# Splitting a load of 127 rows into 112 and 15 in a fused attention, Fourier and MLP kernel

## The chip, the cores and the metric

The kernel runs on one NeuronCore of a Trainium2 chip. The metric is the device time of one execution in microseconds (us). TensorE is called PE, VectorE DVE, ScalarE ACT, GpSimd POOL. SyncE, called SP, computes nothing here: it issues most of the DMA transfers, one after the other, in the order in which the program lists them. A transfer is carried out by the core's 16 DMA engines, and a semaphore tells the waiting engines when it has landed.

## The reference, cut to what matters

Three blocks follow each other: attention with a learned relative bias, a Fourier mixing block with an MLP, and a gated block. Only the hand-over from attention to the Fourier transform is touched here.

```python
attn = softmax(q @ k.T / 8 + bias) @ v                 # B=4, 8 heads, S=576, D=64
x = attn.transpose(0, 2, 1, 3).reshape(4, 576, 512)
X = np.fft.fft(np.fft.fft(x, axis=1), axis=2)          # over the sequence, then over the width
u = x + np.real(X)
un = (u - mean(u)) / sqrt(var(u) + 1e-6)
x = u + relu(un @ w_ch1) @ w_ch2                       # 512 -> 2048 -> 512
# then: w_in, a normalisation, a 576 x 576 spatial product, a gate, w_out
```

All of it is float32 with split products (a high and a low part), so a matrix product takes several matmuls.

## The kernel before, in words

The program runs in stages: the bias (up to about 130 us), attention (130 to 390 us), the Fourier stage (388 to 459 us), the MLP with its normalisation, and the gated block, which ends at 1096 us.

Attention takes the 16 pairs (4 batches, 4 pairs of heads) in order, two pairs at a time in nine steps `d`, each step two units of 128 query rows. A step computes scores on PE (L417), adds the bias on DVE, takes the exponential on ACT (L453), and then turns the probabilities round so that they can be multiplied with the values on PE (L519, tile `po`). In odd steps (and the last four) PE turns them (L493). In even steps ACT and POOL make a half-precision copy `hl` (L464, L470) and SP issues a DMA transpose of it (L483, `pt<-hl`), three steps before PE reads the result. SP also issues the loads of `q`, `k` and `v` (L382, tile `raw`) and the stores of the finished rows to a buffer in HBM, `xd[b]`, one of 576 rows by 512 for each batch: `store` issues one transfer for rows 0 to 511 (L569) and two for the last 64 rows (L572).

The Fourier transform of a real sequence over 576 positions needs only sums and differences of row `t` and row `576 - t`, so each batch is loaded from `xd[b]` in such a way that these rows share a partition. `Folds.loads` does this for one batch: POOL writes zeros, and then SP issues six transfers (L748), rows 0 to 127 and 128 to 255 into slots 0 and 1, the 127 rows from 256 into slot 3 from partition 1 on, 128 rows from 383 into slot 4, one row, and the last 64 rows into slot 2. A row is 2048 bytes. The tile is `x` for batch 0, `raw` for batch 1 and `lowb` for batches 2 and 3.

When the loads go out is set in `first_folds`. Batch 0's go out one by one during attention: `after(n)` is called at the end of each step with `n` counted from the last one, and in the steps that `F_STEPS` names it takes one step of the generator. Batch 1's go out together at `n = 0` and batch 2's at `n = 3`. Batch 3's are the operation `load` in the Fourier stage, behind the first three weight loads (L1697, tile `w`); SP has to wait there until the last stores to `xd[3]` have landed.

In the Fourier stage a planner (`Plan.run`) fixes the order of each engine's operations from written-down durations. For each batch DVE makes the sums (L765, L776, L783, "folds"), PE multiplies them with cosines and sines (L878, tile `y`), ACT copies the result out of PSUM (L882), PE applies the second transform (L908, tile `D`), and DVE adds (L918, L926). Between these ACT and DVE also prepare the first MLP weights: ACT scales a weight tile (L1036, `wsq<-w`) as soon as its load has landed, and in ACT's list the first of these stands ahead of two of the copies L882. The planner counts batch 3's load as one operation of 6 us on SP, whatever it is made of.

Of the kernel before, what the change touches and what calls it, by code (L numbers as in the profile page):

```python
# [713 lines left out]
class Folds:  # L714
# [22 lines left out]
    def loads(self, b):  # L737
        nc, x, d = self.nc, self.xs[b], self.xd[b]
        f = slice(1, DM + 1)

        def zeros():
            if b == 0:
                nc.gpsimd.memset(x[64:128, 2], 0.0)
            nc.gpsimd.memset(x[:, 2, 0 : DM + 2 : DM + 1], 0.0)
            nc.gpsimd.memset(x[0:1, 3, f], 0.0)

        def part(p, k, lo, n):
            nc.sync.dma_start(out=x[p : p + n, k, f], in_=d[lo : lo + n])  # L748

        yield zeros  # L750
        for p, k, lo, n in (0, 0, 0, 128), (0, 1, 128, 128), (1, 3, 256, 127), (0, 4, 383, 128), (64, 2, 511, 1), (0, 2, 512, 64):
            yield lambda p=p, k=k, lo=lo, n=n: part(p, k, lo, n)

    def load(self, b):
# [39 lines left out]
def first_folds(folds):  # L794

    todo, loads = [], folds.loads(0)

    def after(n):
        if F_LOAD <= n < 0 and n % 9 in F_STEPS:
            next(loads, int)()  # L800
        if n == 0:
            folds.open()
            todo.extend(folds.steps(0))
        if n in X_LOAD:
            folds.load(1 + X_LOAD.index(n))
        for _ in range(FOLDS.get(n, 0)):
            todo.pop(0)[2]()

    return after
# [1125 lines left out]
```

## Time and profile before

| | us |
|---|---|
| median of 3 runs | 1096.97 (1095.49 to 1101.35) |
| the profiled execution | 1098.06 |
| its span in the trace | 1096.3 |
| PE busy in the span | 1017.9 (93%) |
| DVE, ACT, POOL busy | 692.5, 546.2, 293.6 |

The span is the time between the first and the last instruction in the trace; the execution's own time is 1.76 us longer. The profile page gives each engine's busy time over the whole span, which is an average over stages that have different limits. So the rows further down are taken stage by stage: from the timeline (instructions of one engine in order of time), from tables of busy time by window, and from the chain of waits, which follows the end of the program back to what released each step. A number in square brackets at the end of a timeline row is the idle time of the engine ahead of that row, with what ended it.

### The profile page before, as it was taken

The numbers are of one execution on the slowest core, as the hardware profiler recorded it, in microseconds if no ns is written. First come the engines' busy times: TensorE is split into PE (matmuls) and PEld (weight loads), VectorE is DVE, ScalarE is ACT, GpSimd is POOL, SyncE is SP. The second block draws the span as 40 slices with busy tenths as digits, with TensorE's granted clock in tenths as the row PEclk, the third lists the DMA queues.
The fourth block names the chain that finished last, engine by engine and source line by source line (L and its number), as shares of the span: only waits on it lengthen the run. The fifth ranks groups of instructions, "written<-read, shape, count | busy, mean of one in ns | idle before, by whom it ended". The sixth has DMA issues, their size and how long they took to land.

```text
span 1096.3 us, 25413 instructions
## 1 busy us (share of the span) xinstructions
PE 1017.9 (93%) x10547; PEld 928.3 (85%) x10547; DVE 692.5 (63%) x1812; ACT 546.2 (50%) x1034; POOL 293.6 (27%) x284
## 2 busy tenths in 40 slices
PE   6989888888688979999999999999999999999998
PEld 3777777877678856789999999999999989988897
DVE  5999888888678877877875332433792366261611
ACT  3888698888679734644531121211452234333322
POOL 2767786878569300000000000000003020110000
PEclk7999989999889989999999999999999999999999
DMA  4542057889787641134520000000241000101011
GB/s 165 176 138 83 14 125 160 179 186 161 177 167 152 136 139 42 39 102 135 173 94 1 1 2 1 1 1 20 78 162 28 1 1 1 39 1 49 1 39 48
DMA packets 116167, 88.22 MB, mean 80 GB/s; under 512 B 85840, under 2 KB 96340, under 8 KB 116052
## 3 DMA queue, kind: packets, MB, share of 16 engines
q1 hardware_dynamic: 113184, 79.82, 28.8%
q10 hardware_dynamic: 2724, 5.90, 1.6%
q8 instruction: 82, 1.34, 0.5%
q0 software_dynamic: 144, 0.89, 0.2%
q14 instruction: 33, 0.27, 0.1%
HBM read 57.10 MB, written 9.44 MB: 61 GB/s over the span
## 4 chain that ended last, share of the span: by engine, by line
PE 65%; DVE 14%; POOL 8%; issue 5%; DMA 4%; ACT 3%; SPq 1%; ACTq 0%; POOLq 0%; DVEq 0%
PE h L1360 18%; PE acc L1396 18%; PE psp L1532 5%; PE pu L1507 4%; PE po L1554 4%; POOL hl L470 4%; PE pv L1455 3%; DVE mask L243 2%; PE po L519 2%; DVE bt L320 2%; PE turn L493 2%; PE bps L276 2%; PE sc L417 2%; DMA lowb<-xd 1%; DVE pt L502 1%
## 5 line engine op out<-in xcount | busy, mean ns | idle before, releaser
L1364 ACT ACTIVATE gh<-h 128x256 fp32r<-128x256 f32 x144 | 54.9, 381 | 243.1 <-PE h L1360 239.2
L1365 DVE SCALAR_TENSOR_TENSOR gl<-h,gh 128x256 fp32r<-128x256 f32 x144 | 60.9, 423 | 171.3 <-ACT gh L1364 170.7
L1360 PE MATMUL h<-uh,wh 128*128 128x256 f32 x576 | 161.7, 281 | 2.2 <-DVE gl L1365 2.0
L1396 PE MATMUL acc<-gh,wh 128*128 128x256 f32 x576 | 163.1, 283 | 0.0
L1396 PE MATMUL acc<-gh,wl 128*128 128x256 f32 x576 | 161.1, 280 | 1.4 <-DVE wl L1068 1.4
L1360 PE MATMUL h<-uh,wl 128*128 128x256 f32 x576 | 161.0, 280 | 1.0 <-DVE wl L1068 1.0
L1360 PE MATMUL h<-ul,wh 128*128 128x256 f32 x576 | 160.8, 279 | 0.0
L1396 PE MATMUL acc<-gl,wh 128*128 128x256 f32 x576 | 160.8, 279 | 0.0
L1152 POOL MEMSET w<- 64x288 f32 x2 | 0.7, 334 | 443.3 <-DVE wsq L1049 443.3
L1360 PEld LDWEIGHTS h<-uh,wh 128*128 128x128 f32 x576 | 109.1, 189 | 3.0 <-DVE gl L1365 2.4
L1396 PEld LDWEIGHTS acc<-gh,wl 128*128 128x128 f32 x576 | 108.5, 188 | 1.7 <-DVE wl L1068 1.6
L1360 PEld LDWEIGHTS h<-uh,wl 128*128 128x128 f32 x576 | 108.5, 188 | 1.2 <-DVE wl L1068 1.2
L1396 PEld LDWEIGHTS acc<-gh,wh 128*128 128x128 f32 x576 | 108.9, 189 | 0.4
L1396 PEld LDWEIGHTS acc<-gl,wh 128*128 128x128 f32 x576 | 108.9, 189 | 0.3
L1360 PEld LDWEIGHTS h<-ul,wh 128*128 128x128 f32 x576 | 108.8, 189 | 0.0
L453 ACT ACTIVATE P<-s,mm 128x576 f32<-128x576 f32 x144 | 103.4, 766 | 3.9 <-DVE mm L445 3.6
L519 PE MATMUL po<-vp,pt 128*128 128x65 f16 (+3 forms) x2324 | 85.4, 197 | 8.3 <-DMA pt<-hl 7.0
L519 PEld LDWEIGHTS <-pt 128*128 128x128 f16 (+1 forms) x2324 | 81.9, 102 | 11.9 <-DMA pt<-hl 7.7
L470 POOL TENSOR_TENSOR hl<-P,hl 128x1024 f16<-128x1024 f32 x68 | 86.1, 1287 | 19.2 <-ACT hl L464 12.6
L493 PE MATMUL turn<-ident,P 128*128 128x128 f32 x380 | 58.9, 287 | 28.6 <-DVE pt L502 28.1
L276 PE MATMUL bps<-g,mask 128*128 128x64 f16 x1152 | 63.1, 196 | 16.2 <-DVE lowb L310 8.3
L493 PEld LDWEIGHTS turn<-ident,P 128*128 128x128 f32 x380 | 41.8, 144 | 41.5 <-DVE pt L502 15.8
(256 smaller groups left out, 2598.5 us busy)
## 6 DMA issues: line engine op xcount, KB each, us to landing
w<-in_w_ch SPq DMA_DIRECT2D x32, 512.0 KB
vld<-in_v ACTq DMA_DIRECT2D x16, 320.0 KB
raw<-in_q SPq DMA_DIRECT2D x16, 320.0 KB
raw<-in_v SPq DMA_DIRECT2D x16, 320.0 KB
raw<-in_k SPq DMA_DIRECT2D x16, 288.0 KB
xd<-x SPq DMA_DIRECT2D x16, 256.0 KB
w<-in_w_in SPq DMA_DIRECT2D x8, 512.0 KB
out<-o SPq DMA_DIRECT2D x16, 256.0 KB
```

The lines of the kernel that those rows point to most:

```text
L276: nc.tensor.matmul(out=full(ps, it // 2)[:, it % 2, :, gi], lhsT=ms[gi][:, 128 * it + 64 * (it // 2) :][:, 0:128], rhs=g[:, k], start=(k = ...
L453: nc.scalar.activation(out=P[:, x, 0:S], in_=s, func=AF.Exp, bias=mm[:, 1, x : x + 1], scale=1.0)
L470: nc.gpsimd.tensor_tensor(out=hl[:, :, o : o + c], in0=P[:, :, j : j + c], in1=hl[:, :, j : j + c], op=ALU.subtract)
L493: nc.tensor.transpose(t[:, 128 * k : 128 * k + 128], P[:, 128 * k : 128 * k + 128], ident)
L519: nc.tensor.matmul(out=po[c, t % 4, 0:w], lhsT=pt[:, x, c], rhs=vp[:, j, hh, f : f + w], start=(i == 0), stop=(i == len(seq) - 1),)
L1360: nc.tensor.matmul(out=h, lhsT=st[:, q], rhs=mv[:, k], start=(n == 0), stop=(n == 11))
L1364: nc.scalar.activation(out=gh, in_=h, func=AF.Relu)
L1365: nc.vector.scalar_tensor_tensor(out=gl, in0=h, scalar=0.0, in1=gh.bitcast(F32), op0=ALU.max, op1=ALU.subtract)
L1396: nc.tensor.matmul(out=acc[x, d // 2][:, d % 2], lhsT=st[:, q], rhs=mv, start=(e == 0 and d % 2 == 0 and n == 0), stop=(e == NF - 1 and d ...
L1507: nc.tensor.matmul(out=p[:, 0:CH], lhsT=st[:, q], rhs=mv[:, kk, e], start=(n == 0), stop=(n == 11))
L1532: nc.tensor.matmul(out=p[:, 0:CH], lhsT=st, rhs=mv, start=(n == 0), stop=(n == len(seq) - 1))
L1554: nc.tensor.matmul(out=p, lhsT=st[:, f, c], rhs=mv, start=(n == 0), stop=(n == 11))
```

## The change

The list of transfers in `Folds.loads` gets one more entry. The 127 rows from row 256 on go as 112 rows (256 to 367, into partitions 1 to 112) and 15 rows (368 to 382, into partitions 113 to 127). The bytes, their places and the other transfers stay.

```diff
         yield zeros
-        for p, k, lo, n in (0, 0, 0, 128), (0, 1, 128, 128), (1, 3, 256, 127), (0, 4, 383, 128), (64, 2, 511, 1), (0, 2, 512, 64):
+        parts = (0, 0, 0, 128), (0, 1, 128, 128), (1, 3, 256, 112), (113, 3, 368, 15), (0, 4, 383, 128), (64, 2, 511, 1), (0, 2, 512, 64)
+        for p, k, lo, n in parts:
             yield lambda p=p, k=k, lo=lo, n=n: part(p, k, lo, n)
```

The order of PE, DVE, ACT and POOL stays as it was. SP gets four more transfers. For batch 0 the generator has one more element, so everything behind the 112 rows goes out one place later. In the middle of attention SP's order was this (`x_71` is batch 0's tile, `xd_74` its buffer in HBM):

```order
L483 DMA_TRANSPOSE pt<-hl 128x18x128
L748 DMA x_71<-xd_74 127x512
L748 DMA x_71<-xd_74 128x512
L483 DMA_TRANSPOSE pt<-hl 128x18x128
L382 DMA raw<-in_k 128x576
L382 DMA raw<-in_q 128x640
L569 DMA xd_75<-x 128x4x128
L572 DMA xd_75<-x 64x64 x2
L483 DMA_TRANSPOSE pt<-hl 128x18x128
L382 DMA raw<-in_v 128x640
L748 DMA x_71<-xd_74 1x512
```

With the change the same place reads:

```order
L483 DMA_TRANSPOSE pt<-hl 128x18x128
L748 DMA x_71<-xd_74 112x512
L748 DMA x_71<-xd_74 15x512
L483 DMA_TRANSPOSE pt<-hl 128x18x128
L382 DMA raw<-in_k 128x576
L382 DMA raw<-in_q 128x640
L569 DMA xd_75<-x 128x4x128
L572 DMA xd_75<-x 64x64 x2
L483 DMA_TRANSPOSE pt<-hl 128x18x128
L382 DMA raw<-in_v 128x640
L748 DMA x_71<-xd_74 128x512
L483 DMA_TRANSPOSE pt<-hl 128x18x128
```

The 15 rows stand where the next 128 rows stood; those go out some steps later in the single row's place, and the single row and the last 64 rows move back in the same way.

At the end of attention and the start of the Fourier stage SP's order was this (`xd_76` and `xd_77` are the buffers of batches 2 and 3, `w` the weight tiles):

```order
L748 DMA lowb<-xd_76 128x512 x2
L748 DMA lowb<-xd_76 127x512
L748 DMA lowb<-xd_76 128x512
L748 DMA lowb<-xd_76 1x512
L748 DMA lowb<-xd_76 64x512
L569 DMA xd_77<-x 128x4x128
L572 DMA xd_77<-x 64x64 x2
L1697 DMA w_8645<-in_w_ch 128x1024
L1697 DMA w_8648<-in_w_ch 128x1024
L1697 DMA w_8650<-in_w_ch 128x1024
L748 DMA lowb<-xd_77 128x512 x2
L748 DMA lowb<-xd_77 127x512
```

With the change:

```order
L748 DMA lowb<-xd_76 128x512 x2
L748 DMA lowb<-xd_76 112x512
L748 DMA lowb<-xd_76 15x512
L748 DMA lowb<-xd_76 128x512
L748 DMA lowb<-xd_76 1x512
L748 DMA lowb<-xd_76 64x512
L569 DMA xd_77<-x 128x4x128
L572 DMA xd_77<-x 64x64 x2
L1698 DMA w_8648<-in_w_ch 128x1024
L1698 DMA w_8651<-in_w_ch 128x1024
L1698 DMA w_8653<-in_w_ch 128x1024
L748 DMA lowb<-xd_77 128x512 x2
```

Here nothing changes places; each load has one transfer more, in the place of the 127 rows.

## Rows read from the trace of the kernel before

**Rows 1.** Busy time by window: Fourier stage, then everything behind it.
```profile
398.20:459.00 60.80, 55.97 (x256) 38.94 (x255) 42.53 (x80) 30.59 (x60) 0.00 (x0) 0.94 0.23 74
459.00:1096.30 637.30, 624.42 (x4751) 600.77 (x4749) 316.61 (x768) 208.35 (x487) 32.84 (x31) 1.00 0.13 42
```
**Rows 2.** Same view (PE, PEld, DVE, ACT, POOL, granted clock, DMA share, GB/s).
```profile
412.00:414.00 2.00, 2.00 (x9) 1.51 (x8) 0.12 (x1) 0.81 (x2) 0.00 (x0) 0.83 0.82 217
416.00:420.50 4.50, 4.50 (x23) 2.63 (x21) 0.71 (x2) 0.96 (x2) 0.00 (x0) 1.00 0.07 25
274.00:278.00 4.00, 1.45 (x16) 1.05 (x12) 3.06 (x8) 3.90 (x7) 2.93 (x4) 1.00 0.07 25
```
**Rows 3.** Timeline of SP in attention: start, duration, line, operation, tiles, count.
```profile
236.75 0.57 SPq L748 DMA_DIRECT2D x<-xd  x1
...
263.67 2.76 SPq L483 DMA_TRANSPOSE pt<-hl  x1
266.48 3.80 SPq L748 DMA_DIRECT2D x<-xd  x2
270.45 9.22 SPq L483 DMA_TRANSPOSE pt<-hl  x1
```
**Rows 4.** Timeline of PE in attention, around its longest wait.
```profile
269.97 1.03 PE L519 MATMUL po<-vp,pt 128*128 128x65 f16 x28 [0.28 <-DMA pt<-hl]
...
272.53 1.08 PE L519 MATMUL po<-vp,pt 128*128 128x65 f16 x30
...
281.76 1.71 PE L519 MATMUL po<-vp,pt 128*128 128x65 f16 x28 [6.31 <-DMA pt<-hl]
...
286.26 1.14 PE L519 MATMUL po<-vp,pt 128*128 128x65 f16 x30
```
**Rows 5.** Timeline of PE: the same matmul of four nine-step rounds in turn.
```profile
229.65 0.38 PE L417 MATMUL sc<-kh,qh 128*128 128x288 f32 x1
...
260.55 0.38 PE L417 MATMUL sc<-kh,qh 128*128 128x288 f32 x1
...
297.74 0.38 PE L417 MATMUL sc<-kh,qh 128*128 128x288 f32 x1
...
330.05 0.38 PE L417 MATMUL sc<-kh,qh 128*128 128x288 f32 x1
```
**Rows 6.** Timeline of SP from the end of attention on.
```profile
383.57 10.48 SPq L748 DMA_DIRECT2D lowb<-xd  x6
394.14 0.53 SPq L569 DMA_DIRECT2D xd<-x  x1
...
397.82 5.41 SPq L1697 DMA_DIRECT2D w<-in_w_ch  x3
...
405.20 5.53 SPq L748 DMA_DIRECT2D lowb<-xd  x1
```
**Rows 7.** The chain of waits, 385 to 500 us: start, duration, what.
```profile
394.14 9.86 DMA xd<-x
...
405.20 15.74 DMA lowb<-xd
```
**Rows 8.** Timelines of DVE (first three) and ACT (last), Fourier stage.
```profile
391.75 0.68 DVE L548 TENSOR_TENSOR x<-po,ri 128x512 f32<-128x512 f32 x1
...
403.00 1.23 DVE L765 TENSOR_TENSOR lowb<-lowb 128x1024 f32<-128x1024 f32 x1 [4.75 <-DMA lowb<-xd]
...
421.13 1.22 DVE L765 TENSOR_TENSOR lowb<-lowb 128x1024 f32<-128x1024 f32 x1 [4.43 <-DMA lowb<-xd]
...
405.36 0.66 ACT L1036 ACTIVATE wsq<-w 128x512 f32<-128x512 f32 x1 [7.56 <-DMA w<-in_w_ch]
```
**Rows 9.** Timeline of PE, Fourier stage.
```profile
406.38 3.27 PE L878 MATMUL y<-tt,F 128*128 128x290 f32 x6 [3.50 <-ACT y L882]
409.44 3.72 PE L908 MATMUL D<-y,fs 128*128 128x290 f32 x8
...
415.93 2.12 PE L908 MATMUL D<-y,fs 128*128 128x290 f32 x8
...
426.95 1.74 PE L878 MATMUL y<-tt,F 128*128 128x290 f32 x6
```

## The prediction

> **What bounds the kernel now.** I read the windows by stage first, then the timelines of SP and PE in the two stretches where the loads of L748 go out, then the chain of waits. Behind 459 us PE is busy 624.4 of 637.3 us [rows 1], and nothing there reads the loaded rows: that part can only move as a whole. What can be won lies ahead of it, where PE waits.
>
> The windows show what the 127 rows do. In 416 to 420.5 us, when batch 3's load is under way, the DMA engines are busy 7% of their time and move 25 GB/s, and in 274 to 278 us, after batch 0's, the same [rows 2]. One of 16 engines is 6.25%. So in these stretches one engine works alone, at 25 GB/s. 127 rows of 2048 bytes are 260,096 bytes: at 25 GB/s 10.4 us. While transfers of 128 rows pass, between 412 and 414 us, the share is 0.82 and the rate 217 GB/s. I conclude that the 127 rows go through one engine in a single line, and that whatever else has a part on that engine stands behind them.
>
> Two stretches show the price. In attention SP issues the 127 rows at 266.48 us, and the two transfers there take 3.80 us of its time, against 0.57 for a plain one; the DMA transpose behind them holds SP for 9.22 us, against 2.76 for the one before [rows 3]. PE then stands 6.31 us for a transposed tile [rows 4]. At the start of the Fourier stage the chain of waits runs through a store of 9.86 us and a load of 15.74 us, with nothing but a little issue between them [rows 7]. The store was issued at 394.14 us, behind the six transfers of batch 2's load, which took SP 10.48 us [rows 6], though the rows it stores were ready at 391.75 + 0.68 = 392.43 us [rows 8].
>
> **The change part by part.** Durations are those of the profiled execution, 1098.06 us; the median is 1.09 us lower, and I subtract the same gain from it.
>
> First, how the two new transfers go. No row shows 112 or 15 rows. On one engine 112 rows would take 112 x 2048 bytes / 25 GB/s = 9.2 us, on sixteen a sixteenth, 0.6 us. The nearest rows are the transfers of 128 rows, spread out, and 112 is a multiple of 16 as 128 is; I take 0.6 us. The 15 rows take 1.2 us on one engine and 0.1 us on fifteen, and neither matters below.
>
> The Trainium skill says so outright, in "DMA: Bandwidth & Descriptors", section "Why a DMA increments its semaphore by 16 and not by 1": a transfer is split over the largest number of engines, up to 16, that divides its slowest dimension, so 127 partitions get one, and by the same rule 112 get 16 and 15 get 15. The trace agrees for 127 (a share of 0.07). The same page's "Rules for kernel authors" speaks against this change: two transfers to disjoint parts of the partitions are not worth it, since both share the 16 engines, and one transfer should be used. By that rule the time would stay at 1097 plus four more issues; the 25 GB/s of rows 2 is why I give it little.
>
> Attention, batch 0. The wait of 6.31 us goes, and with it the slow clock behind it: from 281.76 to 286.26 us PE does in 4.50 us what it does from 269.97 to 272.53 in 2.56 us [rows 4], 1.94 us more. Together 8.25 us is the upper end. The lower end comes from the length of a round, taken at the same matmul: 30.90, 37.19 and 32.31 us [rows 5]. Against the longer neighbour the disturbed one is 4.9 us too long, against the mean of both 5.6. Half way between 5.6 and 8.25 I take 6.9 us. What is late next is what sets the ordinary rounds, PE, ACT and POOL by turns.
>
> What the change adds there: one issue, at most 0.6 us of SP by the plain transfer in rows 3. Batch 0's later parts move one place back, ahead of other transposes. Each costs SP what it cost in its old place, and they land long before the Fourier stage reads them. The 0.6 us lie beside POOL's and ACT's work on the next transpose's input, since a transpose holds SP for only 2.76 us and one comes every second step, of some 3.5 us (a ninth of a round); uncovered they would cost 0.6 us.
>
> Fourier stage, batches 1 to 3. In the changed kernel seven transfers of batch 2 take SP about 7 x 0.57 = 4.0 us instead of 10.48, so SP is ready before the last rows are (392.43 us). The three stores and three weight issues follow until about 396 us; batch 3's seven transfers are out at about 401 and landed at about 403. DVE comes to batch 2's first fold right after batch 1's last, at about 398.3 us, instead of 403.00: its wait of 4.75 us goes. Its wait of 4.43 us for batch 3 [rows 8] goes too, since DVE cannot be there before 408 (421.13 less both waits and the slow stretch below), and the data are. ACT's wait of 7.56 us for the first weights shrinks to almost nothing, because the weight load is issued some 3.5 us earlier and has no part behind a line of 127 rows.
>
> What this is worth is decided on PE, which is busy in nearly all of the rest of the stage. There its wait of 3.50 us goes (it came from the copy L882 that stood behind ACT's wait), and the slow clock behind it: 3.27 instead of 1.74 us for six matmuls, 3.72 instead of 2.12 for eight [rows 9], 3.13 us in all. That is 6.63 us. The upper end is DVE's two waits, 9.18 us, if PE's smaller waits behind DVE close as well; the lower end is PE's wait alone, 3.50 us, if the clock falls anyway. I take half way between 6.63 and 9.18, 7.9 us. PE then bounds the stage: it is busy 55.97 of 60.80 us [rows 1], and the 4.83 us left over and the 3.13 us make 7.96, about what I take. The four added issues lie on SP, which then waits for the stores and not they for it.
>
> Sum: 6.9 + 7.9 = 14.8 us. 1098.06 - 14.8 = 1083.3 for a profiled execution, 1096.97 - 14.8 = 1082.2 for the median. I forecast 1082.
>
> **The rivals.**
> *Attention takes its gain back.* Rounds are set by several engines in turn, and the two behind the stall may be short only because others had caught up. For it: ordinary rounds differ by 1.4 us too [rows 5], so something else than the stall has its say. Against: the neighbours on both sides are alike [rows 5]. Then only the Fourier stage gains: 1096.97 - 7.9 = 1089.
> *The Fourier stage takes its gain back,* because the weights or batch 3's rows still come late (SP issues everything in one line). For it: SP's three weight issues take 5.41 us [rows 6]. Against: that time was spent behind the same engine. Then 1096.97 - 6.9 = 1090.
> *The change does not do what it says:* 112 rows go through one engine as well, 9.2 us instead of 10.4. Rows 2 do not exclude it. Between 1092 and 1099, say 1097.
> *Slower: SP is held by the number of transfers it has outstanding, not by the one engine.* The place is the transfer behind the 127 rows: it holds SP 5.53 us [rows 6] and, in attention, the greater part of 3.80. If a new transfer is held whenever a few are open, a seventh in each load is one more hold: 3.80 - 0.57 = 3.2 us ahead of the transpose in attention and 5.53 us ahead of the stores and in batch 3's load, 3.2 + 2 x 5.53 = 14 us less what lies beside other work, about 11: 1108. It decides from the point where a transfer behind the 15 rows holds SP for more than 3 us. Against it: transfers one behind another elsewhere take 0.6 us each.
>
> **How the numbers follow.** Forecast 0.73, attention alone failing 0.10, the Fourier stage alone failing 0.08, no effect 0.05, slower 0.04. The likeliest case's own bounds are 1096.97 - 17.4 = 1079.5 (both upper ends) and 1096.97 - 8.4 = 1088.6 (both lower ends). The range takes in the first two rivals and, below, another 3.5 us for waits of PE that the rows do not tell apart: 1076 to 1090. A measurement of this kernel can tell about 0.5%, 5.5 us, from no change. Below 1091.5 lie the first three cases, 0.91, less 0.01 for their edges: faster 0.90. The case of no effect and the edges give 0.06 for the same, and the last 0.04 is slower.
>
> **What would show it.** In the profile of the changed kernel no window of some microseconds should be left with a DMA share of 0.07 and 25 GB/s around the loads; no DMA transpose should hold SP over 4 us; the third round in rows 5 should last about 30 us; DVE's two waits for `lowb<-xd` should be gone and ACT's for `w` be under 2 us; PE's first MLP matmul, at 459 us before, should start about 15 us earlier, and the time from there to the end should be the same. I am wrong if the 112 rows still show 25 GB/s, if the transfer behind the 15 rows holds SP, or if the MLP's start moves by less than 9 us.

## The result and the profile after

The changed kernel takes 1076.78 us (median of 4 runs, 1075.67 to 1081.53) against 1096.23 us (4 runs, 1094.3 to 1101.35) measured beside it. The ratio is 0.9832 with a 95% interval of 0.9808 to 0.9856, so 15.8 to 21.0 us less. The forecast was 1082, range 1076 to 1090: the right direction and the right places, but the gain was about 19 us where 14.8 were forecast.

The lines of SP in attention that answer to [rows 3], timeline view:

```profile
263.01 2.78 SPq L483 DMA_TRANSPOSE pt<-hl  x1
265.84 1.10 SPq L748 DMA_DIRECT2D x<-xd  x2
267.12 3.19 SPq L483 DMA_TRANSPOSE pt<-hl  x1
```

The two transfers take 1.10 us in place of 3.80, and the transpose behind them holds SP for 3.19 us in place of 9.22. The longest of all 34 transposes holds it for 3.79. PE's timeline, which answers to [rows 4], has no wait for a transposed tile any more, except 0.28 us that were there before:

```profile
269.32 1.03 PE L519 MATMUL po<-vp,pt 128*128 128x65 f16 x28 [0.28 <-DMA pt<-hl]
...
271.88 1.08 PE L519 MATMUL po<-vp,pt 128*128 128x65 f16 x30
...
274.66 1.02 PE L519 MATMUL po<-vp,pt 128*128 128x65 f16 x28
...
277.34 1.08 PE L519 MATMUL po<-vp,pt 128*128 128x65 f16 x30
```

The same matmul of four rounds in turn, as in [rows 5]:

```profile
228.72 0.38 PE L417 MATMUL sc<-kh,qh 128*128 128x288 f32 x1
...
259.90 0.38 PE L417 MATMUL sc<-kh,qh 128*128 128x288 f32 x1
...
288.77 0.38 PE L417 MATMUL sc<-kh,qh 128*128 128x288 f32 x1
...
319.16 0.38 PE L417 MATMUL sc<-kh,qh 128*128 128x288 f32 x1
```

The rounds last 31.18, 28.87 and 30.39 us, where they lasted 30.90, 37.19 and 32.31: 8.32 us less in the disturbed one.

At the end of attention, SP's timeline answers to [rows 6]:

```profile
370.91 3.28 SPq L748 DMA_DIRECT2D lowb<-xd  x7
381.71 0.38 SPq L569 DMA_DIRECT2D xd<-x  x1
382.14 1.17 SPq L572 DMA_DIRECT2D xd<-x  x2
383.41 1.47 SPq L1698 DMA_DIRECT2D w<-in_w_ch  x3
384.97 4.02 SPq L748 DMA_DIRECT2D lowb<-xd  x7
```

Seven transfers take 3.28 us where six took 10.48, and the last stores go out at 381.71 us, as soon as DVE has their rows (381.00 + 0.68). While the weights and batch 3's load pass, rows of the windows view (PE, PEld, DVE, ACT, POOL, granted clock, DMA share, GB/s), to be set beside the 25 GB/s of [rows 2]:

```profile
384.50:390.50 6.00, 6.00 (x19) 3.57 (x19) 5.90 (x10) 2.66 (x6) 0.00 (x0) 0.75 0.99 355
392.00:394.00 2.00, 2.00 (x10) 1.55 (x9) 0.86 (x2) 1.29 (x4) 0.00 (x0) 1.00 1.05 321
394.25:394.50 0.25, 0.25 (x3) 0.20 (x2) 0.25 (x2) 0.25 (x1) 0.00 (x0) 1.00 0.01 0
```

The DMA engines are busy to the end of the load and then idle: no tail at a share of 0.07 is left behind it. None of the 28 issues of the loads (L748) holds SP for more than 0.59 us; the longest of the 24 before was 5.53.

DVE's two folds (L766, which was L765) and ACT's first weight tile, which answer to [rows 8]; none of them waits for a transfer:

```profile
387.43 1.22 DVE L766 TENSOR_TENSOR lowb<-lowb 128x1024 f32<-128x1024 f32 x1
...
399.03 1.22 DVE L766 TENSOR_TENSOR lowb<-lowb 128x1024 f32<-128x1024 f32 x1
```
```profile
387.74 0.68 ACT L1037 ACTIVATE wsq<-w 128x512 f32<-128x512 f32 x1
```

PE, which answers to [rows 9]. Behind it windows of the whole Fourier stage, from its first matmul to the MLP's first one (before, then after), and of what follows it (after; [rows 1] has it before):

```profile
384.05 9.55 PE L879 MATMUL y<-tt,F 128*128 128x290 f32 x30 [1.47 <-DVE F L784]
393.44 2.12 PE L909 MATMUL D<-y,fs 128*128 128x290 f32 x8
```
```profile
388.30:459.08 70.78, 63.95 (x293) 44.98 (x291) 52.36 (x98) 34.90 (x69) 0.00 (x0) 0.93 0.25 80
377.55:439.35 61.80, 59.79 (x294) 43.31 (x291) 52.34 (x98) 34.78 (x69) 0.00 (x0) 0.97 0.23 76
439.40:1075.10 635.70, 622.51 (x4750) 599.08 (x4748) 316.78 (x768) 208.27 (x487) 32.86 (x31) 1.00 0.13 42
```

The wait of 3.50 us inside the matmuls of `y` is gone, and the eight matmuls of `D` take 2.12 us instead of 3.72. The stage takes 61.80 us instead of 70.78: 8.98 us. The MLP starts 19.7 us earlier, where the prediction said about 15. What follows lasts 635.8 us instead of 637.2.

So the 21.1 us between the two spans (1096.3 and 1075.1) are 8.3 in the disturbed round, 9.0 in the Fourier stage, 1.9 in the round behind the disturbed one, 1.4 behind the Fourier stage and about 0.5 elsewhere. The last three are told apart from the change further down.

### The profile page after: what moved, and what is told of

Read it like the earlier page. It is cut to its first block, busy times and chain, and to the rows that moved or that the text cites. A ratio compares the mean times of both kernels' runs of the same rounds, so it can differ in the third digit from the quotient of the medians.

```text
span 1075.1 us, 25420 instructions
## 1 busy us (share of the span) xinstructions
PE 1006.4 (94%) x10547; PEld 920.5 (86%) x10547; DVE 692.6 (64%) x1812; ACT 546.2 (51%) x1034; POOL 293.5 (27%) x284
## 4 chain that ended last, share of the span: by engine, by line
PE 67%; DVE 15%; POOL 8%; issue 4%; DMA 3%; ACT 2%; ACTq 0%; POOLq 0%; DVEq 0%
PE h L1361 18%; PE acc L1397 18%; PE psp L1533 5%; PE pu L1508 4%; POOL hl L470 4%; PE po L1555 4%; PE pv L1456 3%; PE y L879 3%; DVE mask L243 2%; PE po L519 2%; PE sc L417 2%; DVE bt L320 2%; PE bps L276 2%; DMA pt<-hl 2%; PE turn L493 2%
## 5 line engine op out<-in xcount | busy, mean ns | idle before, releaser
L493 PE MATMUL turn<-ident,P 128*128 128x128 f32 x380 | 57.9, 284 | 29.6 <-DVE pt L502 29.2
```

The lines of the kernel that those rows point to most:

```text
L493: nc.tensor.transpose(t[:, 128 * k : 128 * k + 128], P[:, 128 * k : 128 * k + 128], ident)
```

## The experiments

**Two halves of the change.** The first kernel splits batch 0 alone, the second batches 1 to 3 alone.

```diff
-        parts = (0, 0, 0, 128), (0, 1, 128, 128), (1, 3, 256, 112), (113, 3, 368, 15), (0, 4, 383, 128), ...
+        mid = ((1, 3, 256, 112), (113, 3, 368, 15)) if b == 0 else ((1, 3, 256, 127),)   # second kernel: b > 0
+        parts = (0, 0, 0, 128), (0, 1, 128, 128), *mid, (0, 4, 383, 128), (64, 2, 511, 1), (0, 2, 512, 64)
```

> Only batch 0's 127 rows go as 112 and 15; batches 1 to 3 keep the 127 rows. One-engine theory: the attention part alone, 8.3 us of the disturbed round plus up to 2 us of the slow clock in the round behind it: 1086 to 1089 against 1096.5; the Fourier stage keeps its waits of 4.75 and 4.43 us. Rival (attention's rounds would take the gain back in the end, the whole gain is the Fourier stage's): 1095 to 1097.

Measured: 1086.66 us, ratio 0.9925 (0.9893 to 0.9957). DVE keeps its two waits:

```profile
392.22 1.23 DVE L767 TENSOR_TENSOR lowb<-lowb 128x1024 f32<-128x1024 f32 x1 [5.05 <-DMA lowb<-xd]
...
410.11 1.23 DVE L767 TENSOR_TENSOR lowb<-lowb 128x1024 f32<-128x1024 f32 x1 [4.75 <-DMA lowb<-xd]
```

The disturbed round lasts 28.9 us and the Fourier stage, from first matmul to first matmul, 70.84.

> Only batches 1 to 3 are split; batch 0 keeps its 127 rows and its order in attention. One-engine theory: the Fourier stage alone, 9.0 us: 1087 to 1089, PE's wait of 6.3 us in attention stays, and the gains of this run and of the one with batch 0 alone add up to that of the change (18 to 20 us). Rival (one shared cause, such as a clock that stays up once a stall is gone): the two gains overlap or do not add up by more than 3 us.

Measured: 1085.36 us, ratio 0.9926 (0.9901 to 0.9950). PE keeps the long wait in attention, and the Fourier stage lasts 61.79 us:

```profile
281.09 1.70 PE L519 MATMUL po<-vp,pt 128*128 128x65 f16 x28 [6.94 <-DMA pt<-hl]
```

The two gains, 0.75% and 0.74% or 8.2 and 8.1 us, come to 16.3 against the 18.4 us of the change by its ratio. Each has an interval of some 3 us to either side, so they add up as far as this can tell. Neither half is taken back, which disposes of the first two rivals.

**One engine, or merely too long a transfer?** 113 is a prime number; 126 divides by 14 but not by 16.

```diff
-(1, 3, 256, 112), (113, 3, 368, 15)
+(1, 3, 256, 113), (114, 3, 369, 14)       # third kernel
+(1, 3, 256, 126), (127, 3, 382, 1)        # fourth kernel
```

> The 127 rows go as 113 and 14: as many transfers as in the change, nearly the same sizes, but 113 is a prime number and 112 is not. One-engine theory: 113 rows still go through one engine, 113 x 2048 bytes / 25 GB/s = 9.3 us instead of 10.4, the stalls stay and get about 1 us shorter each: 1091 to 1096, windows with a DMA share of 0.07. Rival (splitting as such helps, since no transfer is long or since a second one gets other engines): 1076 to 1078 as with 112 and 15.

Measured: 1095.53 us, ratio 0.9991 (0.9968 to 1.0015): no change. One row more or less in the first part makes the whole difference. Windows, SP's transpose, and PE's and DVE's waits of this kernel:

```profile
274.00:276.00 2.00, 1.53 (x16) 1.12 (x14) 1.83 (x5) 1.88 (x4) 2.00 (x3) 1.00 0.07 26
```
```profile
270.34 8.66 SPq L483 DMA_TRANSPOSE pt<-hl  x1
```
```profile
281.11 1.70 PE L519 MATMUL po<-vp,pt 128*128 128x65 f16 x28 [5.58 <-DMA pt<-hl]
```
```profile
399.01 1.23 DVE L766 TENSOR_TENSOR lowb<-lowb 128x1024 f32<-128x1024 f32 x1 [2.61 <-DMA lowb<-xd]
...
416.81 1.23 DVE L766 TENSOR_TENSOR lowb<-lowb 128x1024 f32<-128x1024 f32 x1 [5.07 <-DMA lowb<-xd]
```

The one engine is back (a share of 0.07, 26 GB/s), and so are the waits. In the trace the line is shorter by about as much as 14 rows fewer should make it (the round lasts 36.0 us, the Fourier stage 68.3, against 37.2 and 70.8); in the timed runs that does not show.

> The 127 rows go as 126 and 1. One-engine theory in the form that the count of engines is the largest number up to 16 that divides the rows: 126 gives 14 engines, 9 rows each, 0.75 us: 1076 to 1079. Rival (only multiples of 16 are spread, everything else goes through one engine): 126 rows in one line of 10.3 us: 1095 to 1099.

Measured: 1079.36 us, ratio 0.9860 (0.9843 to 0.9878). No transpose holds SP for more than 3.59 us, and DVE does not wait for a transfer. So a multiple of 16 is not needed. The Trainium skill's rule for the number of engines ("DMA: Bandwidth & Descriptors", section "Why a DMA increments its semaphore by 16 and not by 1") gives 14 for 126, 1 for 113 and 16 for 112. The three kernels agree as far as one engine against many goes; that it is 14 and not 16 for 126 rows no run here shows. The Trainium skill's rule against two transfers to disjoint partition halves, from the same page's "Rules for kernel authors", takes for granted that each of them is spread over all 16 engines. The change gains by two transfers (0.9832) because the single one was not spread and its parts are; in the third kernel (0.9991) the greater part still is not.

**Was it the order?** The 127 rows stay whole, but batch 0's later parts go out one place later, as in the change.

```diff
             yield lambda p=p, k=k, lo=lo, n=n: part(p, k, lo, n)
+            if b == 0 and n == 127:
+                yield lambda: None
```

> The 127 rows stay whole in all batches; in attention batch 0's parts behind them go out one place later, as in the change. One-engine theory: the transpose still stands behind the line, so PE's wait of about 6 us stays: 1092 to 1097. Rival (attention's gain came from moving the 128 rows away from the place ahead of the transpose): about 1087.

Measured: 1095.91 us, ratio 0.9996 (0.9978 to 1.0014). SP in the same place:

```profile
266.37 0.47 SPq L748 DMA_DIRECT2D x<-xd  x1
267.65 11.43 SPq L483 DMA_TRANSPOSE pt<-hl  x1
279.12 0.59 SPq L382 DMA_DIRECT2D raw<-in_k  x1
```

Without the 128 rows in between the transpose is issued 2.8 us earlier and is held 2.2 us longer: it ends at 279.08 us instead of 279.67. Its end follows the line that was begun at 266.4 us in both, and PE still waits 5.75 us for the transposed tile. Moving the 128 rows away gains nothing.

**Which of the late loads?** Batch 3 alone, and batches 2 and 3, with the condition of the first diff set to `b == 3` and `b > 1`.

> Only batch 3 is split. Theory: batch 2's line still delays the stores, the first weights and its own rows, so DVE's wait of 4.75 us, ACT's of about 7.5 us and PE's of 3.5 us with the slow clock behind it stay and only the wait of 4.43 us goes, which PE partly covers: 1092 to 1095. Rival (batch 3's line alone is what the chain of waits shows as 15.74 us and carries the Fourier stage's gain): 1087 to 1089.

Measured: 1092.54 us, ratio 0.9971 (0.9949 to 0.9992), Fourier stage 67.06 us. DVE's first wait and ACT's stay, DVE's second is gone:

```profile
404.07 1.23 DVE L767 TENSOR_TENSOR lowb<-lowb 128x1024 f32<-128x1024 f32 x1 [4.17 <-DMA lowb<-xd]
...
416.69 1.22 DVE L767 TENSOR_TENSOR lowb<-lowb 128x1024 f32<-128x1024 f32 x1
```
```profile
406.43 0.66 ACT L1038 ACTIVATE wsq<-w 128x512 f32<-128x512 f32 x1 [7.73 <-DMA w<-in_w_ch]
```

> Only batches 2 and 3 are split, 0 and 1 keep the 127 rows. Theory (a line costs what stands behind it on SP and on that engine): batch 1's line runs from about 374 to 387 us, while DVE is busy with attention's last tiles and batch 0's folds, and is over before the last rows are stored, so it costs little: within 2 us of the run with batches 1 to 3 split, 1086 to 1089. Rival (each of the three lines costs its hold of SP of some 4 us): 1090 to 1092.

Measured: 1085.90 us, ratio 0.9908 (0.9880 to 0.9937), Fourier stage 61.80 us, as with all three split. Batch 1's line does hold SP (its six transfers take 7.50 us), but nothing waits for what is late: the last rows to be stored are not ready until later. In the Fourier stage, then, batch 3's line costs 3.7 us by the trace, batch 2's and batch 3's together 9.0, batch 1's nothing.

**The same fault elsewhere.** In the chain of waits of the changed kernel the longest piece ahead of attention is another transfer: `win`, a table of 4 rows of the bias stage, each broadcast to 32 partitions, in one transfer whose outermost dimension is 4. It is under way from 9 to 12 us, at a DMA share of 0.26 and 94 GB/s: four engines of sixteen, at about 23 GB/s for each.

```profile
9.00:12.00 3.00, 1.70 (x10) 0.68 (x8) 0.00 (x0) 2.07 (x4) 0.00 (x0) 1.00 0.26 94
```
```profile
1.68 12.68 DMA win<-in_c_win
```

```diff
-    nc.scalar.dma_start(
-        out=win, in_=io["c_win"].rearrange("j (a i) -> j a i", a=1).to_broadcast([4, HID, WLEN])
-    )
+    for j in range(4):
+        nc.scalar.dma_start(out=win[HID * j : HID * j + HID], in_=io["c_win"][j : j + 1].to_broadcast([HID, WLEN]))
```

> The change, and beside it one more load of the same kind: the bias stage's table win (4 rows, each broadcast to 32 partitions) goes as four transfers of 32 partitions instead of one whose outermost dimension is 4. In the changed kernel that one transfer takes 12.68 us in the chain of waits and DVE stands 6.16 us for it. Theory (the count of engines divides the outermost dimension, so 4 of 16 work): with 32 as outermost dimension it lands by about 8 us and the time falls by 4 to 6 us against the changed kernel: 1071 to 1073. Rival (the transfer is long because the broadcast source or its 588 KB are slow, on however many engines): no gain, 1076 to 1078.

Measured: 1070.88 us, ratio to the kernel before 0.9766 (0.9746 to 0.9786). It was then run again in the same rounds as the changed kernel, together with a kernel that has this edit alone.

> The changed kernel again, on the same chip and in the same rounds as the next two, so that they can be compared: 0.983 of the kernel before, about 1077.

> The change and the four loads of win again. If its gain over the change is what its trace shows at the first matmul that every round of attention begins with (2.3 us) and no more, the ratio to the changed kernel is 0.998; if the whole of the first comparison was real, 0.993.

> Only win goes as four loads, the 127 rows stay whole. If the two causes are independent, the gain is that of the win loads over the change, 2 to 7 us: 1090 to 1095 against 1096.5. If the table's late arrival is made up for before attention ends, no gain: 1096.

Measured against the kernel before: the change 0.9837 (0.9813 to 0.9861), the change with the loads of `win` 0.9803 (0.9775 to 0.9832), the loads of `win` alone 0.9948 (0.9928 to 0.9968). Alone, the edit gains 3.5 to 7.9 us. On top of the change the two intervals overlap in this comparison, by 3.7 us in the middle, while in the first one it was 7 us, against a run of the change on another occasion: that it gains there too is likely, its size is open. Two independent gains would give 0.9837 x 0.9948 = 0.9786, which lies inside the measured interval. DVE's wait for `win` in the second run is 1.63 us instead of 6.16, and the table is there 4 us earlier:

```profile
10.44 0.82 DVE L213 TENSOR_SCALAR win<-win,w 128x1148 f32<-128x1148 f32 x1 [1.63 <-DMA win<-in_c_win]
```

With the median of 1074.05 us beside 1077.89 for the change (1070.88 in its first run), this version has the lowest times found.

Four medians lie just outside what was expected of them: batches 1 to 3 by 1.6 us (1085.36 against 1087 to 1089), 126 rows by 0.4, the first run with `win` and batches 2 and 3 by 0.1 each. The second run with `win` came out between its two cases, at 0.996 of the changed kernel. None of this decides between a theory and its rival.

## Why the prediction was right, and where it was off

*The 127 rows go through one engine and what has a part there stands behind them.* Right: 113 rows, also on one engine, keep every stall (DVE's first one shorter, 2.61 us instead of 4.75), while 112 and 126 rows lose them all. (The views give the share of time and not which engine worked; that it is one engine is read from a share of one sixteenth.) The rival that the change does not do what it says falls with the DMA shares of 0.99 and 1.05 while batch 3's load passes, and the slower rival with the transfer behind the 15 rows: all seven of batch 2 take 3.28 us together, some 0.5 us each, where it wanted a hold of more than 3 us on one of them.

*Attention: 6.9 us.* This term was sized too small. The step that was off is the lower end, taken from the neighbouring rounds: they are not like the one between them. Undisturbed rounds alternate: in the changed kernel they last 28.9, 31.6, 28.9, 31.2, 28.9, 30.4 and 28.5 us. The four rounds ahead of the stall show it in the kernel before already (29.2, 31.6, 28.9, 30.9). The round in this place lasts 28.9 us in each kernel that loses the stall (the change and its second run, batch 0 alone, 126 rows, both runs with `win`). With the 127 rows whole it lasts 36.2 to 38.8 us in six traces. The direct sum, 6.31 us of waiting and 1.94 us of slow clock, was the better figure: 8.25 forecast as the upper end, 8.32 measured. That they agree to 0.07 us is partly luck, since the stalled round itself differs by up to 2.5 us from trace to trace. The slow clock that the prediction read from durations is there in the windows view: 0.50 granted from 281.76 to 286.26 us, 1.00 from 269.97 to 272.53.

*Fourier stage: 7.9 us.* Nearly right: 8.98 us, close to the upper end of 9.18. DVE's waits of 4.75 and 4.43 us and ACT's of 7.56 went, as said, and PE bounds the stage, busy 59.79 of 61.80 us. DVE comes to batch 3's fold 21.5 us after the stage's first matmul, which in the time of before is 409.8 us; 408 was said. By the two windows of the stage PE's idle time fell by 4.8 us (6.83 to 2.01): the wait of 3.50 us and the smaller ones behind DVE, of which only a part was counted. Its busy time fell by 4.2 us (63.95 to 59.79), where the slow clock was put at 3.13. The figure has luck in it too: with 126 rows, and in both runs with `win`, the stage takes 60.11 us, which would be a gain of 10.7 us, above the upper end. The last section has the reason.

*The rest.* Forecast terms and measured ones differ by 2.5 us (17.3 against 14.8), which is the greater part of the miss by the ratio (18.4). The other 1.9 and 1.4 us of the two traces are not shown to be the change's. In the round behind the disturbed one PE has the same wait of 2.1 us in both traces, and then the granted clock differs (0.69 is a mean over the two levels, 1.00 the upper one alone):

```profile
314.00:322.00 8.00, 5.58 (x63) 4.83 (x64) 5.98 (x17) 7.29 (x11) 5.90 (x5) 0.69 0.89 210
```
```profile
305.00:313.00 8.00, 4.81 (x107) 4.38 (x108) 5.98 (x17) 7.62 (x12) 5.89 (x5) 1.00 0.89 212
```

The first row is the kernel before, the second the changed one. In six other traces with a whole line in batch 0 or 113 rows there, this round lasts 30.9 to 31.5 us, and 30.4 to 31.2 without, so about half a microsecond may be the change's. The part behind the Fourier stage lasts 634.8 to 638.2 us in the traces of all kernels, with and without the change.

*The four added issues cost nothing.* Right: SP has issued batch 2's load by 374.19 us, and the rows that it stores next are ready at 381.68; for batch 3's load no engine waits.

## What to carry to other kernels

In these runs loads of 127 and 113 rows went through one DMA engine and a broadcast with 4 outermost through four, while 112 and 126 rows were spread, as the rule cited above has it. So look for loads with such awkward counts of rows, and for broadcasts with a small count outermost, and cut them into pieces whose count has a large divisor up to 16. In these profiles they show as windows with a DMA share of 0.07 and 25 GB/s (one engine) or 0.26 and 94 GB/s (four). The price need not fall on the rows that come late: in attention it was paid by a transpose issued behind them, and in the Fourier stage in part by stores and weight loads behind them and by SP. So look at what was issued next.

## What was not expected of the hardware

The clock's price for the same wait is not always the same. Near the start of the Fourier stage PE waits 1.47 us for DVE in every kernel that has lost the stalls of this stage, and then does the same 30 matmuls. In the changed kernel, in its second run, with batches 1 to 3 split and with batches 2 and 3 split they take 9.55 us. A window of the changed kernel shows the clock granted at 0.57 in the first 4 us, so at the lower level, 1.2 GHz, for most of that time:

```profile
384.05:388.00 3.95, 3.95 (x9) 2.84 (x10) 3.92 (x7) 0.69 (x3) 0.00 (x0) 0.57 0.88 287
```

With 126 rows and in both runs with `win` they take 7.87 us; in the second run with `win`, whose row stands here, the clock is 1.00 throughout, the 2.4 GHz level:

```profile
378.73 7.87 PE L878 MATMUL y<-tt,F 128*128 128x290 f32 x30 [1.47 <-DVE F L783]
```

That is 1.68 us, the whole difference between Fourier stages of 61.80 and 60.11 us. What decides it was not tried.
